# GpSimd tied to VectorE in a planned kernel: channel attention and a feed-forward block on one core

## The chip, the core and the metric

The kernel runs on one core of one Trainium2 chip. The metric is device time in microseconds, from the run's start to its end; the time before is 2167.81 us, the median of three runs (2167.71 to 2172.11). TensorE does the matrix products, VectorE and ScalarE the element-wise work, GpSimd a few subtractions; SyncE only issues DMAs. In the profile they are PE (its weight loads PEld), DVE, ACT, POOL and SP.

## The reference, cut to what matters

```python
# q, k, v: 4 x 6080 x 256;  w_in: 256 x 2048;  w_out: 2048 x 256, all float32
qn = q / (norm(q, axis=1) + 1e-6); kn = k / (norm(k, axis=1) + 1e-6)
a = softmax(kn.T @ qn / tau)          # 256 x 256 per batch
x = (v @ a).reshape(24320, 256)
h = x @ w_in
g = where(h >= 1, h, where(h <= -1, 0, (h + 1)**2 / 4))
out = g @ w_out
```

The attention is over channels: a batch's 6080 rows meet only in a 256 x 256 matrix.

## The kernel before

**Arithmetic.** `x @ w_in` is never formed with `x`: per batch the kernel multiplies the softmax matrix into `w_in` once and applies the product W to v. Every float32 operand is split in a high part, rounded to fp32r, and a low part, the rest; `mm3` (L588) makes each product of three matmuls. W times v, 256 hidden columns by two blocks of up to 512 tokens, is done as seven products in the manner of Strassen; their sums and differences are made by ScalarE copies (L766, L768), VectorE additions (L771, L775) and, for the pieces of v, GpSimd subtractions (L868 in `make_V`, into the tiles `t`).

**Groups.** The main loop has 192 groups: 4 batches, 6 pairs of token blocks, 8 blocks of 256 hidden columns. A group makes four banks of h; for each, ScalarE saturates (L919) and squares (L923), VectorE takes the maximum with h (L928), which is the activation; then the high part is copied (L943 on ScalarE or L945 on VectorE, as the planner picks) and VectorE subtracts it to give the low part (L947). The results (`g`, `x` in the profile) are what the matmuls with w_out read. In the first of the eight blocks the w_out product is also done with fewer multiplications: four GpSimd subtractions in `combos` (L993) make the sums of the activations that it needs; there are 24 such chains.

**Work beside it.** While one batch runs, the next one's 256 x 256 matrix is summed chunk by chunk: a DMA of q and k rows, a split on ScalarE and VectorE (L597, L598, the tile `kqs`), twelve matmuls of 256 columns, and an addition on VectorE (L615). GpSimd also makes sums of W (L824 in `split_f`) and of w_in (L563). Two PSUM banks (pool Z) serve, in turn, the products of the h chain, the fourth bank of h and the chunk's matmuls: the chunk can begin only when VectorE has read the last of h from its bank (L928).

**What sets the order.** Nothing of the main part is scheduled by the compiler. `op()` records an operation with its engine, a duration, what it reads and writes, and a due time; `Order.run` then plays the whole program through as a plan: at each step it takes the operation that can start first on any engine, the one with the lowest due time among those that can start now, gives it a start, an end and a buffer, and emits it. The emitted order is the order on each engine's queue; across engines only real dependencies are kept, by semaphores. The plan knows that some VectorE operations and the GpSimd ones shut each other out: an operation marked `locks` starts only when the other engine's lock has ended, which is `RELEASE` = 0.14 before the end. Due times come from tables of offsets (`T_PLAIN`, `T_STR`) from the group's 16 units, and from a few numbers in the main loop. In the plan a DMA ends a fixed `LAT` of 3.0 after its bytes have passed a single stream.

Of the kernel before, what the change touches and what calls it, by code (L numbers as in the profile page):

```python
# [11 lines left out]
U32 = mybir.dt.uint32  # L12
# [3 lines left out]
P = 128  # L16
# [35 lines left out]
SOON = 0.3  # L52
AHEAD, RATE = -34.0, 41.78
LATER = -3.46


class Op:
    __slots__ = ("eng", "dur", "fn", "due", "deps", "gates", "bufs", "next", "count", "start", "end", "n", "size",
                 "alts", "slack", "lat", "locks", "table")


class Order:
# [10 lines left out]
    LOAD = 1.29  # L73
    BYTES = 405e3
    FREE = {"PE": 2.0, "ACT": 2.0, "DVE": 1.5, "POOL": 1.5, "SP": 1.2}

    def __init__(self):
        self.ops = []
        self.lock = {"DVE": 0.0, "POOL": 0.0}
        self.table = None  # L80

# [64 lines left out]
    def run(self):  # L146
        free = dict(self.FREE)
        avail = {e: [] for e in self.LAG}
        dma = 0.0
        for o in self.ops:  # L150
# [19 lines left out]
        while left:  # L170
# [82 lines left out]
def pool_us(n):  # L253
# [7 lines left out]
G = 16  # L261
U = 32.22

# [5 lines left out]

LAT = 3.0  # L270
SLACK = 1
# [6 lines left out]
SQ0 = (4, 2)  # L278
RN_SLACK = (1.0, 3.0)
ET_SLACK = (2.0, 3.0)  # L280

# [3 lines left out]
T_PLAIN = {  # L285
    'sat00': 2.98,
    'sq00': -0.31,
    'max00': -2.38,
    'sat01': 7.36,
    'sq01': 3.87,  # L290
    'max01': 15.96,
    'sat11': 31.21,
    'sq11': 16.45,
    'max11': 17.07,
    'sat10': 16.54,
    'sq10': 12.89,
    'max10': 12.97,
    'sq': 9.06,
    'hi0': ((0, 16.38), (1, 16.82)),
    'lo0': ((0, 21.57), (1, 24.39)),  # L300
    'hi1': ((0, 23.28), (1, 23.36)),
    'lo1': ((0, 21.72), (1, 13.19)),
    'o': ((34.97, 38.77, 42.57, 39.06), (24.47, 26.42, 31.77, 20.96)),
}
T_STR = {
    'sat00': 1.98,
    'sq00': -7.92,
    'max00': -4.57,
    'sat01': -9.47,
    'sq01': -2.24,  # L310
    'max01': 50.9,
    'sat11': 26.21,
    'sq11': -0.38,
    'max11': 16.09,
    'sat10': 27.37,
    'sq10': 30.81,
    'max10': -3.19,
    'sq': 44.51,
    'hi0': ((0, -20.66), (1, 35.02)),
    'lo0': ((0, 27.87), (1, 18.19)),  # L320
    'hi1': ((0, 23.08), (1, 11.54)),
    'lo1': ((0, 13.1), (1, 8.58)),
    'sum': (36.44, 30.5, 21.24, 20.85),
    'direct': (17.8, 24.05, 22.11, 13.48),
    'chain': (35.74, 38.29, 60.46),
    'hi2': ((0, 14.57), (1, 40.57)),
    'lo2': ((0, 25.25), (1, 38.89)),
    'hi4': ((0, 44.31),),
    'lo4': ((0, 43.11),),
    'late': -22.72,  # L330
    'early': 23.14,
}
# [10 lines left out]
def channel_attention_moe(ctx: ExitStack, tc: tile.TileContext, kq, kqT, vT, tau, w_in, w_out, outT):  # L343
# [12 lines left out]
    nc = tc.nc  # L356
# [5 lines left out]
    RT = 2  # L362
# [111 lines left out]
    def load(b, src, dst, due, size, gates=(), r=(), slack=0.0):  # L474
        return op("SP", 0.35, lambda: nc.sync.dma_start(out=dst(), in_=src()), r=r, w=[b], due=due, gates=gates,
                  size=size, slack=slack)


    def convert(src, out, dst, due, gates=(), step=0.4, load_due=None, n=1, keep=None):
# [23 lines left out]
        if keep is not None:  # L503
            op("SP", 0.35, lambda: nc.sync.dma_start(out=x_dram[keep], in_=cu()), r=[cb], w=[x_store[keep]], due=due + 20,
               size=128 * 2048)
# [35 lines left out]
    def make_w_in(i, due, gates=(), load_due=None):  # L541
        b = win_buf[0, i] = buf("win")
        convert(w_in[i].rearrange("p a f -> p (a f)"), [b], lambda x: b.ap[:, x].rearrange("p a f -> p (a f)"), due, gates,
                load_due=load_due, keep=i)
        sb_, y, h = i // 4, i // 2 % 2, i % 2
        for ct, j in ((0, V_11), (1, V_21)) if y == 0 else ((1, V_22),):
            op("SP", 0.35, lambda ct=ct, j=j: nc.sync.dma_start(
                out=wop_dram[sb_][:, j, :, h * FF:(h + 1) * FF], in_=b.ap[:, :, ct, :].bitcast(U32)),
               r=[b], w=[wop_store[sb_][j]], due=due + 24, size=128 * 2048)

    def sums_w_in(i, due, gates=()):
# [80 lines left out]
    def softmax(b, due):  # L632
# [81 lines left out]
        else:  # L714
# [17 lines left out]

            op("SP", 3.0, blocks, r=[x], w=[ed], due=due + 8, size=P * 2048, slack=ET_SLACK[0])
            op("SP", 0.7, rows, r=[ed], w=[f], due=due + 8, size=P * 2048, slack=ET_SLACK[1])
# [45 lines left out]
    def make_W7(b, sb_, d, gates=()):  # L780
# [16 lines left out]
        for k, (it, y, h) in enumerate(((0, 0, a), (0, 1, bb), (1, 1, h22), (1, 0, z))):  # L797
            o = buf("u", TB)
            op("ACT", act_us(TB), lambda it=it, h=h, o=o: nc.scalar.mul(o.ap, h.ap, st.rs()[:, it:it + 1]), r=[h, st.col],
               w=[o], due=d + (10, 15, 16, 18)[k])  # L800
            op("SP", 0.35, lambda it=it, y=y, o=o: nc.sync.dma_start(
                out=raw_dram[b][sb_][:, 2 * y:2 * y + 2, it], in_=o.ap.rearrange("p (n f) -> p n f", n=2).bitcast(U32)),
               r=[o], w=[raw_store[b][sb_]], due=d + (10, 15, 16, 18)[k], size=128 * 2048)
# [30 lines left out]
    def split_W(b, i, f, due, parts=((0, NS),), eng="POOL", fview=lambda x: x):  # L834
        w = w_buf[b, 0, i]
        split_f(f, w, due, parts, eng, fview=fview)
        op("SP", 0.35, lambda: nc.sync.dma_start(out=w_dram[b][i], in_=w.ap.bitcast(U32).rearrange("p a j f -> p (a j f)")),
           r=[w], w=[w_store[b][i]], due=due + 24, size=128 * WSZ * 4)
# [204 lines left out]
    def o_ops(g):  # L1043
# [6 lines left out]
        for y in (1, 0):  # L1050
            dues = T_PLAIN["o"][y]
            for ct in range(CT):
# [8 lines left out]
                if i == FP - 1:  # L1061
# [11 lines left out]
                    op("SP", 0.35, lambda yb=yb, ct=ct, c0=c0: nc.sync.dma_start(  # L1073
                        out=outT[ct * P:(ct + 1) * P, c0:c0 + n], in_=yb.ap[:, :n]), r=[yb], due=due + 1,
# [80 lines left out]
    for g, (b, k, i) in enumerate(groups):  # L1155
# [17 lines left out]
        if i == 4 and g + 4 < NG:  # L1173
            make_V(*groups[g + 4][:2], d + 17.46, gate(g), 2.25)
        if b + 1 < B:
# [6 lines left out]
            for c, r0 in enumerate(rows):  # L1182
                if q == lo_ + c * (hi_ - lo_) // len(rows):
                    gram_chunk(b + 1, r0, min(P, (N - r0) // RT), d + 16.08, gate(g))
            for c in range(24):
                if q == SQ0[b > 0] + c * (KP * FP - SOFT_AT - SQ0[b > 0] + 1) // 24:
                    s, r = divmod(c, 2 * NCW)
                    square_piece(b + 1, s, r // NCW, r % NCW, d + 23.68, gate(g))
# [35 lines left out]
```

## Time and profile before

| | |
|---|---|
| median of three runs | 2167.81 us |
| profiled execution, its own time | 2169.51 us |
| its span, first to last instruction | 2167.7 us |
| PE busy, share of the span | 2150.7 us, 99% |
| DVE busy | 1896.2 us, 87% |
| ACT busy | 1635.1 us, 75% |
| POOL busy | 396.1 us, 18% |

A matmul's record runs on after the next has started, so PE's busy time counts a little more than its work. In the timeline a row gives start, duration, engine, line, operation, tiles, shapes and a count of like instructions merged; in square brackets stands the idle time of the engine just before it and what ended it.

### The profile page before, as it was taken

The page shows a single profiled execution, that of the slowest core. Times are in us where ns is not written, and L with a number is a line of the kernel's source. Part 1 is how long each engine was busy: PE and PEld are TensorE (multiplying, and loading weights), DVE is VectorE, ACT ScalarE, POOL GpSimd, SP SyncE. Part 2 cuts the span into 40 slices and gives each one's busy share as a digit, 9 for nine tenths or more (in the row PEclk, how much of TensorE's full clock was granted, in tenths as well). Part 3 has the DMA queues.
Part 4 walks back from the last instruction along what each step waited for, and adds up shares of the span by engine and source line. Part 5 has one row for each costly group of instructions (what it writes and reads, how often), then busy time and mean ns, then how long its engine had stood idle before and what let it go on. Part 6 is the DMA issues. An engine that isn't in the chain of part 4 may idle for free.

```text
span 2167.7 us, 28241 instructions
## 1 busy us (share of the span) xinstructions
PE 2150.7 (99%) x9800; PEld 1783.5 (82%) x9800; DVE 1896.2 (87%) x3017; ACT 1635.1 (75%) x2943; POOL 396.1 (18%) x358
## 2 busy tenths in 40 slices
PE   9999999999999999999999999999999999999999
PEld 7888888788878888888887888888888788888888
DVE  8998889889798888988979889898897998888886
ACT  6687788778688787777868877777787876776775
POOL 0321032121141110111124101011112410110110
PEclk9999999999999999999999999999999999999999
DMA  9854366544755444544566444444457433333331
GB/s 387 302 183 172 134 203 216 170 152 156 233 189 187 160 163 173 191 155 138 175 214 209 172 178 170 153 172 162 142 182 231 143 123 108 119 123 108 118 122 70
DMA packets 123839, 371.47 MB, mean 171 GB/s; under 512 B 17200, under 2 KB 48816, under 8 KB 121136
## 3 DMA queue, kind: packets, MB, share of 16 engines
q1 hardware_dynamic: 123696, 369.67, 48.6%
q8 instruction: 77, 1.26, 0.2%
q14 instruction: 66, 0.54, 0.1%
HBM read 298.84 MB, written 70.78 MB: 171 GB/s over the span
## 4 chain that ended last, share of the span: by engine, by line
PE 88%; DVE 8%; ACT 2%; issue 1%; DMA 1%; SPq 0%; DVEq 0%; ACTq 0%
PE bank L588 86%; DVE x L947 2%; PE bank L1107 2%; DVE u_mem L928 2%; DVE mh_mem L1123 1%; ACT u_mem L919 1%; ACT u_mem L923 1%; DVE x L945 1%; DVE g L947 0%; DVE w_mem L830 0%; DMA raw_mem<-raw_d 0%; DVE mh_mem L775 0%; DMA kq<-kq 0%; DVE u_mem L497 0%; DVE kqs L598 0%
## 5 line engine op out<-in xcount | busy, mean ns | idle before, releaser
L588 PE MATMUL bank<-v,w_mem 128*128 128x512 f32 (+1 forms) x3264 | 861.5, 389 | 1.0 <-DVE bank L771 0.3
L588 PE MATMUL bank<-x,wout 128*128 128x512 f32 (+1 forms) x3195 | 823.4, 388 | 1.6 <-DVE x L947 1.2
L588 PEld LDWEIGHTS bank<-v,w_mem 128*128 128x128 f32 x3264 | 607.4, 188 | 130.2 <-ACT bank L768 4.2
L588 PEld LDWEIGHTS bank<-x,wout 128*128 128x128 f32 x3195 | 597.8, 188 | 125.7 <-DVE x L947 5.6
L919 ACT ACTIVATE u_mem<-bank 128x512 f32<-128x512 f32 (+1 forms) x576 | 341.6, 594 | 316.2 <-PE bank L588 311.3
L928 DVE TENSOR_TENSOR u_mem<-bank,u_mem 128x512 f32<-128x512 f32 (+1 forms) x576 | 390.5, 679 | 167.7 <-ACT u_mem L923 165.1
L923 ACT ACTIVATE u_mem<-u_mem 128x512 f32<-128x512 f32 (+1 forms) x768 | 466.6, 626 | 7.9
L947 DVE TENSOR_TENSOR x<-u_mem,x 128x512 fp32r<-128x512 f32 (+1 forms) x580 | 416.5, 730 | 7.8 <-ACT x L943 1.2
L588 PE MATMUL bank<-g,wout 128*128 128x512 f32 (+1 forms) x1053 | 278.0, 388 | 0.0
L588 PEld LDWEIGHTS bank<-g,wout 128*128 128x128 f32 x1053 | 197.0, 188 | 39.6 <-DVE g L947 0.2
L943 ACT CAST x<-u_mem 128x512 fp32r<-128x512 f32 (+1 forms) x285 | 175.6, 618 | 55.4 <-DVE u_mem L928 45.9
L588 PE MATMUL bank<-x,w_mem 128*128 128x512 f32 (+1 forms) x768 | 211.0, 389 | 0.1
L868 POOL TENSOR_TENSOR t<-raw_mem 128x512 f32<-128x512 f32 (+1 forms) x48 | 67.1, 1398 | 627.6 <-DMA raw_mem<-vT 355.8
L588 PEld LDWEIGHTS bank<-x,w_mem 128*128 128x128 f32 x768 | 142.7, 188 | 32.1 <-ACT bank L768 1.3
L868 POOL TENSOR_TENSOR t<-raw_mem,t 128x512 f32<-128x512 f32 (+1 forms) x48 | 66.4, 1383 | 497.0 <-DVE v L877 383.4
L771 DVE TENSOR_TENSOR bank<-bank,mh_mem 128x512 f32<-128x512 f32 (+1 forms) x198 | 135.8, 686 | 13.7 <-PE bank L588 11.9
L775 DVE TENSOR_TENSOR mh_mem<-bank,mh_mem 128x512 f32<-128x512 f32 (+1 forms) x198 | 134.3, 678 | 14.8 <-PE bank L588 13.0
L928 DVE TENSOR_TENSOR u_mem<-mh_mem,u_mem 128x512 f32<-128x512 f32 (+1 forms) x192 | 140.1, 730 | 2.3 <-ACT u_mem L923 2.3
L945 DVE CAST x<-u_mem 128x512 fp32r<-128x512 f32 (+1 forms) x295 | 129.7, 440 | 10.6 <-DVE u_mem L928 0.9
L947 DVE TENSOR_TENSOR g<-u_mem,g 128x512 fp32r<-128x512 f32 (+1 forms) x188 | 135.6, 731 | 2.1 <-ACT g L943 0.5
L993 POOL TENSOR_TENSOR cc<-u_mem 128x512 f32<-128x512 f32 (+1 forms) x48 | 73.6, 1533 | 301.5 <-DVE u_mem L928 283.6
L919 ACT ACTIVATE u_mem<-mh_mem 128x512 f32<-128x512 f32 (+1 forms) x192 | 119.6, 623 | 7.9 <-DVE mh_mem L775 7.6
(129 smaller groups left out, 2028.7 us busy)
## 6 DMA issues: line engine op xcount, KB each, us to landing
w_mem<-w_d SPq DMA_DIRECT2D x160, 896.0 KB, 4.6
raw_mem<-kqT SPq DMA_DIRECT2D x60, 512.0 KB, 5.4
w_d<-w_mem SPq DMA_DIRECT2D x32, 896.0 KB, 4.4
raw_mem<-kq SPq DMA_DIRECT2D x51, 512.0 KB, 5.3
kq<-kq SPq DMA_DIRECT2D x20, 1024.0 KB, 8.5
raw_mem<-vT SPq DMA_DIRECT2D x40, 512.0 KB, 6.3
outT<-y_mem SPq DMA_DIRECT2D x80, 256.0 KB, 2.1
win_mem<-wop_d SPq DMA_DIRECT2D x21, 512.0 KB, 5.6
```

The lines of the kernel that those rows point to most:

```text
L588: nc.tensor.matmul(out, lhsT=lhs(a), rhs=rhs(c), start=start and m == 0, stop=stop and m == 2, skip_group_check=skip)
L771: op("DVE", dve_us(n), lambda: nc.vector.tensor_tensor(out=bb.ap[:, :n], in0=z.ap[:, :n], in1=m5.ap[:, :n], op=ALU.add), r=[z, m5], w=[bb] ...
L775: op("DVE", dve_us(n), lambda: nc.vector.tensor_tensor(out=h22.ap[:, :n], in0=z.ap[:, :n], in1=m5.ap[:, :n], op=ALU.add), r=[z, m5], w=[h2 ...
L868: op("POOL", pool_us(n), lambda: nc.gpsimd.tensor_tensor(out=tt(x), in0=a(), in1=c(), op=ALU.subtract), r=r, w=[ts[x]], due=due + d, gates ...
L919: op("ACT", act_us(n), lambda: nc.scalar.activation(half_of(u, x, n), h.ap[:, :n], IDENTITY_SAT240, scale=240.0), r=[h], w=[u.parts[x]], t ...
L923: op("ACT", act_us(n * (1 + (x is None))), lambda: nc.scalar.activation(part_of(u, x, n), part_of(u, x, n), AF.Square, bias=0.5, scale=1.0 ...
L928: op("DVE", dve_us(n), lambda: nc.vector.tensor_tensor(out=us(), in0=h.ap[:, :n], in1=us(), op=ALU.max), r=[h], w=[u.parts[x]], h=[u], due ...
L943: op("ACT", act_us(cols), lambda x=x: nc.scalar.copy(part(0, x), part_of(u, x, n)), r=of(u.parts, x), w=of(t.parts, x), h=[u, t], due=due, ...
L945: other=("DVE", dve1_us(cols), lambda x=x: nc.vector.tensor_copy(part(0, x), part_of(u, x, n))))
L947: op("DVE", dve_us(n * (1 + (x is None))), lambda x=x: nc.vector.tensor_tensor(out=part(1, x), in0=part_of(u, x, n), in1=f32(part(0, x)), ...
L993: op("POOL", pool_us(n), lambda out=out, o=o, a=a, x=x, c_=c_, y=y: nc.gpsimd.tensor_tensor(out=half_of(out, o, n), in0=half_of(a, x, n), ...
L1107: nc.tensor.matmul(g.ap[:, it * C:(it + 1) * C], lhsT=rb.ap[:p, k0:k0 + P], rhs=rb.ap[:p, t * 512 + C:t * 512 + 2 * C], start=(r0 == 0 and ...
```

## The change

GpSimd's operations that carry the lock get one dependency more: when the plan places one, it looks among the last 16 placed VectorE operations for the latest one that in the plan has ended by then (0.11 for the signal, 0.02 of tolerance), and the GpSimd instruction is made to wait for that instruction's semaphore. Nothing else is computed; no operation is added or taken away.

The plan's DMA model changes: the stream starts at 2.3, a transfer enters it 1.2 after its issue, ends 0.1 after its bytes, and a load is usable 1.8 later still (`LAND`), where before every transfer ended 3.0 after its bytes; issuing one costs 0.45 on SyncE in place of 0.35. `AHEAD` in the class is this 1.2; the module's `AHEAD`, negative before and after, is another number. With it all due offsets have other values, so the planner lays out other orders and, in a few places, picks ScalarE instead of VectorE for a high-part copy.

```diff
@@ class Order
-    BYTES = 405e3
+    BYTES = 403e3
+    AHEAD = 1.2
@@ run
-        dma = 0.0
+        dma = 2.3
...
             if o.eng == "SP":
-                dma = max(dma, t) + o.size / self.BYTES
-                o.end = dma + LAT + o.slack
+                dma = max(dma, t + self.AHEAD) + o.size / self.BYTES
+                o.end = dma + 0.1 + o.slack
             else:
                 o.end = t + o.lat
-            o.fn()
+            o.out = o.fn()
+            if o.eng == "DVE":
+                self.placed.append(o)
+            elif o.eng == "POOL" and o.locks:
+                done = [d for d in self.placed[-16:] if d.end + self.TO["POOL"] <= o.start + 0.02]
+                if done and self.tie:
+                    self.tie(o.out, done[-1].out)
@@ 
-U = 32.22
+U = 34.28
-LAT = 3.0
+LAND = 1.8
-RN_SLACK = (1.0, 3.0)
-ET_SLACK = (2.0, 3.0)
+RN_SLACK = (1.0, 1.0)
+ET_SLACK = (0.5, 1.0)
@@ T_PLAIN, T_STR (nearly every value; one shown)
-    'max10': 12.97,
+    'max10': 26.77,
@@ load (other DMAs alike: 0.35 to 0.45)
-        return op("SP", 0.35, lambda: nc.sync.dma_start(out=dst(), in_=src()), r=r, w=[b], due=due, gates=gates,
-                  size=size, slack=slack)
+        return op("SP", 0.45, lambda: nc.sync.dma_start(out=dst(), in_=src()), r=r, w=[b], due=due, gates=gates,
+                  size=size, slack=LAND + slack)
@@ main loop
-                softmax(b + 1, d + 27.02)
+                softmax(b + 1, d + 35.96)
+    def tie(later, earlier):
+        tc.add_manual_dep(later.ins, earlier.ins.name, mybir.DependencyInfo(
+            mybir.DependencyClass.Sync, mybir.DependencyReason.DATA), reason="order of GpSimd and VectorE")
+    od.tie = tie
     od.run()
```

On GpSimd, where the first batch's sums of w_in (L563, after the change L570) are followed by a pair of subtractions for the pieces of v (L868, then L875), the queue reads before, with the semaphores that each instruction waits for:

```order
L563 TENSOR_TENSOR raw_mem_93<-raw_mem_93 128x256 [waits DMAHW3_49,DMAHW4_49,DMAHW1_49,Activation_49]
L563 TENSOR_TENSOR raw_mem_93<-raw_mem_93 128x256 [waits Pool_49]
L563 TENSOR_TENSOR raw_mem_93<-raw_mem_93 128x256
L868 TENSOR_TENSOR t0_107<-raw_mem_93 128x512 [waits DMAHW5_49,DMAHW4_49,Activation_49]
L868 TENSOR_TENSOR t1_108<-raw_mem_93,t0_107 128x512 [waits Pool_49]
```

and after the change:

```order
L570 TENSOR_TENSOR raw_mem_93<-raw_mem_93 128x256 [waits DMAHW3_49,DMAHW0_49,DVE_49]
L570 TENSOR_TENSOR raw_mem_93<-raw_mem_93 128x256 [waits DVE_49,Pool_49]
L570 TENSOR_TENSOR raw_mem_93<-raw_mem_93 128x256 [waits DVE_49]
L875 TENSOR_TENSOR t0_107<-raw_mem_93 128x512 [waits DMAHW4_49,DMAHW5_49,DVE_49,Activation_49]
L875 TENSOR_TENSOR t1_108<-raw_mem_93,t0_107 128x512 [waits DVE_49,Pool_49]
```

The sequence is the same; each instruction now also waits for a VectorE instruction (DVE_49). Of GpSimd's 363 instructions 114 waited for VectorE before and 337 do after.

On TensorE, ahead of one chunk of the third batch's 256 x 256 matrix (`kqs`), the queue reads before (bank6 and bank7 are the two Z banks, `x3` at a name's start is a piece of v, a final x3 a count):

```order
L588 MATMUL bank0_117<-x3_1041,w_mem_89 128x512 x3
L588 MATMUL bank7_124<-v5_104,w_mem_89 128x512 x3
L588 MATMUL bank2_119<-g0_98,wout_80 128x512 x3
L588 MATMUL bank6_123<-v0_99,w_mem_89 128x512 x3
L588 MATMUL bank2_119<-g0_98,wout_80 128x512 x3
L588 MATMUL bank4_121<-x1_732,wout_80 128x512 x3
L588 MATMUL bank7_124<-kqs_109 128x256 x12
```

and after the change:

```order
L595 MATMUL bank0_117<-x3_1063,w_mem_89 128x512 x3
L595 MATMUL bank6_123<-v5_104,w_mem_89 128x512 x3
L595 MATMUL bank7_124<-v0_99,w_mem_89 128x512 x3
L595 MATMUL bank2_119<-x0_718,wout_80 128x512 x6
L595 MATMUL bank7_124<-v1_100,w_mem_89 128x512 x3
L595 MATMUL bank0_117<-v2_101,w_mem_89 128x512 x3
L595 MATMUL bank6_123<-kqs_109 128x256 x12
```

Between the last product that fills the bank (bank7 from v5 before, bank6 from v5 after) and the chunk that needs it empty stand 12 matmuls before and 15 after.

## Rows read from the trace of the kernel before

**Rows 1.** The page, section 1: busy time and share of the span

```profile
PE 2150.7 (99%) x9800; PEld 1783.5 (82%) x9800; DVE 1896.2 (87%) x3017; ACT 1635.1 (75%) x2943; POOL 396.1 (18%) x358
```

**Rows 2.** Windows: busy time in each stretch (PE, PEld, DVE, ACT, POOL), clock, DMA

```profile
0.00:60.00 60.00, 56.11 (x232) 46.26 (x233) 46.86 (x60) 36.15 (x41) 5.28 (x13) 0.94 0.98 389
...
60.00:2165.00 2105.00, 2094.54 (x9570) 1737.25 (x9568) 1849.37 (x2958) 1598.94 (x2902) 390.79 (x345) 1.00 0.48 165
```

**Rows 3.** Waits of the weight loads, 60 to 2165: total, times, longest

```profile
PEld bank L588 <- DVE u_mem L928: 11.6, 17, 2.3
PEld bank L588 <- DVE x L947: 9.5, 18, 0.9
PEld bank L588 <- ACT bank L768: 5.5, 17, 0.5
PEld bank L588 <- DVE mh_mem L775: 5.3, 15, 0.7
PEld bank L588 <- DVE bank L771: 4.1, 13, 0.7
```

**Rows 4.** The page, section 5: matmuls of one kind, mean ns of one

```profile
L588 PE MATMUL bank<-x,wout 128*128 128x512 f32 (+1 forms) x3195 | 823.4, 388 | 1.6 <-DVE x L947 1.2
```

**Rows 5.** Timeline ahead of the longest stop, at 390.5

```profile
380.75 4.51 POOL L563 TENSOR_TENSOR raw_mem<-raw_mem 128x256 f32<-128x256 f32 x4 [17.96 <-DMA raw_mem<-x_d]
...
385.22 1.30 POOL L868 TENSOR_TENSOR t<-raw_mem 128x512 f32<-128x512 f32 x1
385.29 1.51 DVE L945 CAST x<-u_mem 128x512 fp32r<-128x512 f32 x1
...
386.41 2.20 PE L588 MATMUL bank<-x,wout 128*128 128x512 f32 x9
386.60 1.35 POOL L868 TENSOR_TENSOR t<-raw_mem,t 128x512 f32<-128x512 f32 x1
386.72 1.77 DVE L928 TENSOR_TENSOR u_mem<-mh_mem,u_mem 128x512 f32<-128x512 f32 x1
...
390.53 1.69 PE L588 MATMUL bank<-kqs 128*128 128x256 f32 x12 [1.92 <-DVE u_mem L928]
```

**Rows 6.** DVE by line and form: busy, mean ns of one

```profile
L928 DVE TENSOR_TENSOR u_mem<-bank,u_mem 128x512 f32<-128x512 f32 x480 | 328.0, 685 | 126.5 <-ACT u_mem L923 124.1
...
L928 DVE TENSOR_TENSOR u_mem<-mh_mem,u_mem 128x512 f32<-128x512 f32 x160 | 119.4, 746 | 0.8 <-ACT u_mem L923 0.8
...
L945 DVE CAST x<-u_mem 128x512 fp32r<-128x512 f32 x242 | 107.7, 446 | 8.8 <-DVE u_mem L928 0.9
```

**Rows 7.** Timeline ahead of the stops at 736.8 and 738.0

```profile
732.48 1.30 POOL L868 TENSOR_TENSOR t<-raw_mem 128x512 f32<-128x512 f32 x1 [23.88 <-DMA raw_mem<-vT]
...
733.86 1.30 POOL L868 TENSOR_TENSOR t<-raw_mem,t 128x512 f32<-128x512 f32 x1
733.89 1.82 DVE L928 TENSOR_TENSOR u_mem<-mh_mem,u_mem 128x512 f32<-128x512 f32 x1
...
736.83 0.73 PE L588 MATMUL bank<-x,wout 128*128 128x512 f32 x2 [0.27 <-DVE x L947]
...
738.03 0.74 PE L588 MATMUL bank<-kqs 128*128 128x256 f32 x4 [0.47 <-DVE u_mem L928]
```

**Rows 8.** Timeline: a GpSimd subtraction issued while VectorE is busy

```profile
611.68 0.68 DVE L928 TENSOR_TENSOR u_mem<-bank,u_mem 128x512 f32<-128x512 f32 x1
...
612.28 0.68 DVE L947 TENSOR_TENSOR x<-u_mem,x 128x512 fp32r<-128x512 f32 x1
612.44 1.67 POOL L993 TENSOR_TENSOR cc<-u_mem 128x512 f32<-128x512 f32 x1 [2.88 <-DVE u_mem L928]
...
612.88 2.19 DVE L830 TENSOR_TENSOR w_mem<-raw_mem,w_mem 128x896 fp32r<-128x896 f32 x1
```

**Rows 9.** Waits for GpSimd's results, whole span

```profile
ACT x L943 <- POOL u_mem L993: 6.4, 10, 0.7
...
ACT x L943 <- POOL cc L993: 4.9, 7, 1.1
```

More of the change, by code (lines that the diff above doesn't have):

```diff
@@ L52 @@
 SOON = 0.3
-AHEAD, RATE = -34.0, 41.78
-LATER = -3.46
+AHEAD, RATE = -25.72, 44.15
+LATER = -3.74
 class Op:
     __slots__ = ("eng", "dur", "fn", "due", "deps", "gates", "bufs", "next", "count", "start", "end", "n", "size",
-                 "alts", "slack", "lat", "locks", "table")
+                 "alts", "slack", "out", "lat", "locks", "table")
 class Order:
@@ L79, in __init__ @@
         self.lock = {"DVE": 0.0, "POOL": 0.0}
-        self.table = None
+        self.table, self.placed, self.tie = None, [], None
     def cost(self, eng, dur, r):
@@ L285 @@
 T_PLAIN = {
[L286 to L296, printed above, removed]
-    'max10': 12.97,
[L298 to L303, printed above, removed]
+    'sat00': -1.82,
@@ L304 @@
+    'sq00': 7.34,
+    'max00': -3.51,
+    'sat01': 3.03,
+    'sq01': 4.32,
+    'max01': 13.39,
+    'sat11': 26.31,
+    'sq11': 5.68,
+    'max11': 12.73,
+    'sat10': 11.93,
+    'sq10': 11.5,
+    'max10': 26.77,
+    'sq': 2.38,
+    'hi0': ((0, 16.19), (1, 16.64)),
+    'lo0': ((0, 21.5), (1, 24.47)),
+    'hi1': ((0, 23.81), (1, 23.93)),
+    'lo1': ((0, 20.3), (1, 10.11)),
+    'o': ((35.98, 38.77, 42.56, 39.06), (24.57, 18.78, 31.77, 22.42)),
 }
 T_STR = {
-    'sat00': 1.98,
-    'sq00': -7.92,
@@ L308 @@
[L308 to L331, printed above, removed]
+    'sat00': 4.47,
+    'sq00': -8.11,
+    'max00': -3.57,
+    'sat01': -5.72,
+    'sq01': -1.84,
+    'max01': 51.23,
+    'sat11': 26.79,
+    'sq11': 3.65,
+    'max11': 16.69,
+    'sat10': 23.02,
+    'sq10': 26.77,
+    'max10': 1.12,
+    'sq': 42.09,
+    'hi0': ((0, -15.43), (1, 29.89)),
+    'lo0': ((0, 26.14), (1, 17.69)),
+    'hi1': ((0, 21.32), (1, 11.52)),
@@ L332 @@
+    'lo1': ((0, 17.42), (1, 11.92)),
+    'sum': (32.85, 29.56, 19.16, 18.24),
+    'direct': (17.8, 24.05, 20.89, 13.71),
+    'chain': (36.35, 47.54, 66.55),
+    'hi2': ((0, 15.89), (1, 43.57)),
+    'lo2': ((0, 28.81), (1, 37.59)),
+    'hi4': ((0, 44.87),),
+    'lo4': ((0, 42.97),),
+    'late': -22.54,
+    'early': 22.32,
 }
@@ L503, in convert @@
         if keep is not None:
-            op("SP", 0.35, lambda: nc.sync.dma_start(out=x_dram[keep], in_=cu()), r=[cb], w=[x_store[keep]], due=due + 20,
+            op("SP", 0.45, lambda: nc.sync.dma_start(out=x_dram[keep], in_=cu()), r=[cb], w=[x_store[keep]], due=due + 20,
                size=128 * 2048)
@@ L569, in sums_w_in @@
         for a in range(2):
-            op("SP", 0.35, lambda a=a: nc.sync.dma_start(
+            op("SP", 0.45, lambda a=a: nc.sync.dma_start(
                 out=wop_dram[sb_][:, 0:NS:2, a, h * FF:(h + 1) * FF],
@@ L731, in rows @@
                                       in_=eT_dram[b][jt * P:(jt + 1) * P].rearrange("p (t c) -> p t c", t=CT))
-            op("SP", 3.0, blocks, r=[x], w=[ed], due=due + 8, size=P * 2048, slack=ET_SLACK[0])
+            op("SP", 3.9, blocks, r=[x], w=[ed], due=due + 8, size=P * 2048, slack=ET_SLACK[0])
             op("SP", 0.7, rows, r=[ed], w=[f], due=due + 8, size=P * 2048, slack=ET_SLACK[1])
@@ L836, in split_W @@
         split_f(f, w, due, parts, eng, fview=fview)
-        op("SP", 0.35, lambda: nc.sync.dma_start(out=w_dram[b][i], in_=w.ap.bitcast(U32).rearrange("p a j f -> p (a j f)")),
+        op("SP", 0.45, lambda: nc.sync.dma_start(out=w_dram[b][i], in_=w.ap.bitcast(U32).rearrange("p a j f -> p (a j f)")),
            r=[w], w=[w_store[b][i]], due=due + 24, size=128 * WSZ * 4)
@@ L1173, in channel_attention_moe @@
         if i == 4 and g + 4 < NG:
-            make_V(*groups[g + 4][:2], d + 17.46, gate(g), 2.25)
+            make_V(*groups[g + 4][:2], d + 15.28, gate(g), 1.82)
         if b + 1 < B:
@@ L1183, in channel_attention_moe @@
                 if q == lo_ + c * (hi_ - lo_) // len(rows):
-                    gram_chunk(b + 1, r0, min(P, (N - r0) // RT), d + 16.08, gate(g))
+                    gram_chunk(b + 1, r0, min(P, (N - r0) // RT), d + 17.42, gate(g))
             for c in range(24):
```

8 lines of the change are left out of this document (4 added, 4 removed).

## The prediction

> **What bounds the kernel now.** I read the page's busy times first: TensorE is busy for 99% of the span, VectorE for 87%, GpSimd for 18% [rows 1]. The matmuls are the same before and after, so only the time in which TensorE has none can move. Second, the windows say how much that is: up to 60 us TensorE lacks 3.9 us, and from 60 to 2165 us it is idle for 2105.00 - 2094.54 = 10.5 us [rows 2]. That understates the loss. One matmul's record is 388 ns long [rows 4], but nine in a row take 2.20 us [rows 5], so the next starts after (2.20 - 0.39) / 8 = 0.226 us, and a stop hides its first 0.16 us under the record before it. Third, the waits of the weight loads give the number of stops: the five largest rows hold 80 waits and 36.0 us [rows 3]. So the matmul stream loses about 10.5 + 80 x 0.16 = 23 us after the start. That is an upper bound on the gain as long as the first 60 us stay, about 1.1% of the time; the kernel is one long stream of matmuls with some 80 short stops.
>
> Who makes the stops is in the same rows: VectorE's four of the five hold 30.5 of 36.0 us [rows 3]. It is not late for want of speed on average; the question is what makes it late there. The timeline ahead of the longest stop shows it [rows 5]. GpSimd's four sums of w_in begin when a load lands, 18 us of idling ended, and the pair of subtractions for v follows at once, at 385.22 and 386.60. Beside the first, a VectorE cast takes 1.51 us where its kind takes 0.45 on the mean [rows 6]; beside the second, a maximum takes 1.77 where 0.75 is the mean [rows 6]. Each ends about when the subtraction does. Together VectorE is 2.1 us late, and the chunk that waits for it leaves TensorE idle for 1.92 us, 2.1 with the hidden part. At 732 to 738 us the picture is the same: the pair begins when its load lands, the maximum beside its second half takes 1.82 us, and two stops follow, 0.27 and 0.47 us idle, 1.1 with twice 0.16 [rows 7]. The maximum that reads a PSUM bank shows no such stretch: 685 ns on the mean over 480 [rows 6]. So what shuts the two engines out of each other is SBUF traffic, one of two at a time, and the stops are where GpSimd's turn falls just ahead of a VectorE result that TensorE needs.
>
> **The change part by part.** *The ties.* They add a wait on VectorE to some 220 GpSimd instructions, and each adds no busy time. Behind a waiting GpSimd instruction only GpSimd's queue stands; it is busy for 18% [rows 1], and of its consumers only ScalarE's copies are seen waiting, 6.4 and 4.9 us in 17 waits [rows 9]. So I cost the waits themselves at nothing; if that cover is gone, the price is the first rival's. What the ties take away is a GpSimd operation running before its place in the plan, where a load or a finished GpSimd operation releases it. They can't take away one that comes late because its load is late; GpSimd's queue at the first place shows the same instructions in the same order, with DVE_49 added to each.
>
> *The DMA model.* It moves no transfer by itself; it moves where the plan thinks that a load lands, and with it where GpSimd's turn falls. Both places above begin with a landing [rows 5, 7], so a plan that has it right puts VectorE's needed result on the right side of the pair. A wrong one costs what it costs now.
>
> *The new due times.* They change the order on TensorE, ScalarE and VectorE nearly everywhere. The one place where I can read the gain off the order is the chunk's bank: 12 matmuls stood between filling and needing it, 12 x 0.226 = 2.7 us, and now 15, 3.4 us. The stop there was 1.1 us in two parts [rows 7]; 0.7 us more room takes away most of the second, which is 0.63 with its hidden part. Other places get other room, and new tight ones are possible. The eight casts that move from VectorE to ScalarE give VectorE 8 x 0.45 = 3.6 us of 1896, which I leave out.
>
> *The sum.* What the edit is worth lies between nothing, or less if it makes new stops, and the 23 us of all stops. The waits of the kind that a GpSimd turn lengthens directly or through the queue, the maximum's (L928) and the low part's (L947), are 21.1 of 36.0 us, 59% [rows 3]; of 23 us that is 13.5. GpSimd's subtractions don't vanish, 390.8 us of them [rows 2] still take the port, and an order that is right in the plan still meets late loads. I take three quarters of the 13.5, since both stops that I followed have a cause that the change addresses: 10 us. That quarter is a choice, and both ends stay in the range. The first 60 us keep their order on TensorE nearly row for row, so I leave their 3.9 us, and the end of the program, alone. Against its own time the profiled execution would go from 2169.5 (span 2167.7 and 1.8 around it) to 2159.5; the median shown is 2167.8, 1.7 lower, so I forecast 2157.8 us, 0.46% less. A difference under 0.2%, 4.3 us, can't be told from none here.
>
> **What a tie can't order.** At 612 us GpSimd starts 0.08 us after VectorE's maximum has ended (611.68 + 0.68), but VectorE's own next operation is already recorded from 612.28; GpSimd takes 1.67 instead of the 1.30 of the undisturbed pair [rows 7], so it first waits some 0.4 us, and then the VectorE operation behind takes 2.19 us [rows 8]. The two take turns. A tie to an operation that has just ended releases GpSimd at this very point, and the race with the next VectorE operation stays. The Trainium skill, "SBUF — State Buffer", section "Who interferes with whom", has the rule behind it: the shared port pair is an exclusive lock, whoever issues first holds it for the whole instruction, the other blocks. By that rule the tied instruction, woken later than VectorE goes on by itself, lets one VectorE operation through first; the trace agrees in this row.
>
> **The rivals.** *First, slower: the chains of sums stretch.* The 24 chains of four subtractions (L993) can run back to back today, 0.08 us apart as the pair does [rows 7]. Tied, each of the last three may wait for one VectorE operation more, 0.7 us [rows 6], so a chain ends up to 2.1 us later. ScalarE's copies already wait in 17 places for these results [rows 9]; if half of the delay in each of the 24 chains gets through the copies and low parts to TensorE, that is 24 x 1.05 = 25 us, if a third of that half, 8. It decides from 0.42 us per chain, where it eats the 10. For it: the copies wait now. Against it: the longest of those waits is 1.1 us, and GpSimd idles four fifths of the time. I price it at 8 us over before: 2176.
>
> *Second, no change: the stops move.* VectorE is 87% busy, each GpSimd operation still takes its turn, and a new order has its own tight places. For it: nearly every due time is new, and 12 matmuls of room still stand ahead of other chunks. A fifth of the 13.5 would stay: 2.7 us, 2165.
>
> *Third, more: VectorE always goes first.* If a tied operation loses the race every time and GpSimd's pairs no longer fall together, all of VectorE's share goes, 30.5 / 36.0 of 23 us = 19.5: 2148. Against it: in the row at 612 us GpSimd's turn came one operation later and the next VectorE operation paid 1.1 us [rows 8]. The Trainium skill's rule on the lock, above, speaks against it as well: GpSimd too keeps the pair once it has it.
>
> *Fourth, the ties do nothing* because GpSimd is already behind the plan: where loads land late, the tie is met before it counts. Then only the new order is left, and the time is the second rival's.
>
> **How the numbers follow.** The forecast has 0.57, the first rival 0.15, the second and fourth together 0.18, the third 0.10. The forecast's own range is 2152 to 2163, from all of the 13.5 us and some to a third of it. Of the second and fourth, 0.14 lies within 0.2% and 0.04 below. So faster by over 0.2%: 0.57 + 0.10 + 0.04 = 0.71; within 0.2%: 0.14; slower: 0.15. The range of 8 in 10 takes in the no-change case and leaves out most of the first rival and the far half of the third: 2149 to 2170.
>
> **What would show it.** Right: TensorE's idle time from 60 us on falls from 10.5 to about 6 us; the waits for L928 and L947 in the weight loads' table fall from 35 to under 20; the chunk stops of 0.5 us and more are gone; GpSimd's subtractions list VectorE as what ended their idle time. The DMA step is right if no long stop begins with a landing. Wrong: stops of 1 us behind a stretched VectorE operation stay as many; or copies (L943, then L950) wait much more than 11 us for GpSimd, which is the first rival; or TensorE's idle time falls and the time does not, which would mean that I have the wrong loss. The forecast fails if the time is above 2163.5.

## The result, and the profile after

The changed kernel takes 2145.22 us (median, 2144.74 to 2147.03); the kernel before took 2169.95 us beside it (2167.71 to 2172.11). The ratio is 0.9888 [0.9871, 0.9905]: 24.7 us faster, where 10 were forecast, and below the range. The profiled execution took 2147.03 us with a span of 2145.2, 22.5 less than the span before.

The page of the kernel after, section 1 (answers to [rows 1]); after it, from section 4, the shares of the chain that ended last.

```profile
PE 2133.9 (99%) x9800; PEld 1787.2 (83%) x9800; DVE 1866.1 (87%) x3009; ACT 1627.2 (76%) x2951; POOL 402.5 (19%) x358
...
PE 95%; DVE 2%; DMA 1%; ACT 1%; issue 0%; POOL 0%; SPq 0%; DVEq 0%
```

The windows show when the time was won. As the two programs end 22 us apart, I take a stretch that lies inside both, 60 to 2140 us. Kernel before, columns as in [rows 2]:

```profile
60.00:2140.00 2080.00, 2070.40 (x9460) 1716.67 (x9459) 1832.29 (x2929) 1587.40 (x2880) 390.79 (x345) 1.00 0.48 167
```

Kernel after, the start too:

```profile
0.00:60.00 60.00, 54.95 (x235) 45.48 (x236) 47.66 (x61) 36.22 (x41) 5.28 (x13) 0.97 0.98 390
60.00:2140.00 2080.00, 2077.30 (x9560) 1740.62 (x9559) 1817.82 (x2948) 1590.45 (x2909) 397.23 (x345) 1.00 0.48 167
```

In the same 2080 us TensorE does 100 matmuls more. At 2080 / 9560 = 0.218 us each that is 21.8 of the 22.5 us. So these 21.8 us are stops of the stream, at a granted clock of 1.00 in both kernels. The rest is 3 more matmuls in the first 60 us, 0.7 us; there the clock was 0.94 before and 0.97 after, so that part may belong to the execution and not to the change. TensorE's idle time goes from 9.6 to 2.7 us.

The weight loads' waits of the kernel after, 60 to 2142 us (total, times, longest), answer to [rows 3]:

```profile
PEld bank L595 <- ACT bank L775: 5.0, 13, 1.8
PEld bank L595 <- DVE x L954: 1.7, 3, 0.8
PEld bank L595 <- DVE u_mem L935: 1.4, 7, 0.3
PEld bank L595 <- DVE mh_mem L782: 0.6, 3, 0.2
PEld bank L595 <- DVE bank L778: 0.2, 1, 0.2
```

Lines have moved by 7: L588 is L595 now, L928 is L935, L947 is L954. ScalarE's row stands almost as it stood (5.5 us in 17 waits, then 5.0 in 13); VectorE's four rows, 30.5 us in 63 waits, are 3.9 in 14.

VectorE's forms of the kernel after (busy, mean ns of one), against [rows 6]:

```profile
L935 DVE TENSOR_TENSOR u_mem<-bank,u_mem 128x512 f32<-128x512 f32 x480 | 327.7, 685 | 125.3 <-ACT u_mem L930 119.4
L935 DVE TENSOR_TENSOR u_mem<-mh_mem,u_mem 128x512 f32<-128x512 f32 x160 | 110.8, 693 | 3.2 <-ACT u_mem L930 3.2
L952 DVE CAST x<-u_mem 128x512 fp32r<-128x512 f32 x218 | 92.9, 427 | 7.7 <-PE bank L595 0.5
```

The maximum that reads a PSUM bank has its 685 ns as before; the one that reads SBUF alone falls from 746 to 693 ns, so most of its long meetings with GpSimd are gone.

What ended GpSimd's idle time ahead of the subtractions for v, in the kernel before (total, times, longest):

```profile
POOL t L868 <- DVE v L877: 511.3, 37, 29.1
POOL t L868 <- DMA raw_mem<-vT: 355.8, 17, 48.9
```

and in the kernel after:

```profile
POOL t L875 <- DVE v L884: 397.9, 37, 26.6
POOL t L875 <- DVE bank L778: 320.1, 13, 29.9
POOL t L875 <- DMA raw_mem<-vT: 77.8, 2, 48.7
```

Seventeen times the landing of the piece's own load let GpSimd go; now twice. Where the landing ended the wait before, mostly a VectorE operation that the subtraction reads nothing from ends it now (`DVE bank L778`): that is the tie at work.

The longest stop that is left, timeline of the kernel after (start, duration, idle time before and its releaser):

```profile
1043.48 2.49 POOL L831 TENSOR_TENSOR sf_mem<-sf_mem 128x128 f32<-128x128 f32 x4 [15.54 <-DMA sf_mem<-e_d]
...
1046.00 0.94 ACT L835 CAST eT<-sf_mem 128x896 fp32r<-128x896 f32 x1 [1.98 <-POOL sf_mem L831]
1046.85 0.55 ACT L775 COPY bank<-bank 128x480 f32<-128x480 f32 x1
...
1047.45 0.92 PE L595 MATMUL bank<-x,w_mem 128*128 128x480 f32 x3 [1.33 <-ACT bank L775]
```

GpSimd's sums wait for a landing, ScalarE's cast waits 1.98 us for them, and the bank that TensorE needs stands behind that cast in ScalarE's queue. No tie makes a landing earlier.

### The profile page after: what moved, and what is told of

It reads as the page before. It is cut to its first block, busy times and chain, and to the rows that moved or that the text cites. A ratio compares the mean times of both kernels' runs of the same rounds, so it can differ in the third digit from the quotient of the medians.

```text
span 2145.2 us, 28485 instructions
## 1 busy us (share of the span) xinstructions
PE 2133.9 (99%) x9800; PEld 1787.2 (83%) x9800; DVE 1866.1 (87%) x3009; ACT 1627.2 (76%) x2951; POOL 402.5 (19%) x358
## 4 chain that ended last, share of the span: by engine, by line
PE 95%; DVE 2%; DMA 1%; ACT 1%; issue 0%; POOL 0%; SPq 0%; DVEq 0%
PE bank L595 94%; DVE mh_mem L1130 1%; DMA kq<-kq 1%; PE bank L1114 1%; DMA raw_mem<-w_out 0%; DVE u_mem L504 0%; ACT u_mem L930 0%; DVE x L954 0%; DVE v L884 0%; DVE u_mem L507 0%; ACT u_mem L926 0%; DVE wout L514 0%; DVE u_mem L500 0%; POOL sf_mem L831 0%; ACT y_mem L1129 0%
## 5 line engine op out<-in xcount | busy, mean ns | idle before, releaser
L595 PE MATMUL bank<-v,w_mem 128*128 128x512 f32 (+1 forms) x3264 | 839.1, 388 | 0.7 <-ACT bank L775 0.7
L595 PE MATMUL bank<-x,wout 128*128 128x512 f32 (+1 forms) x3159 | 794.8, 388 | 0.0
L595 PEld LDWEIGHTS bank<-v,w_mem 128*128 128x128 f32 x3264 | 610.1, 188 | 124.4 <-ACT bank L775 2.7
L595 PEld LDWEIGHTS bank<-x,wout 128*128 128x128 f32 x3159 | 591.1, 188 | 117.9 <-DVE x L954 0.2
L935 DVE TENSOR_TENSOR u_mem<-bank,u_mem 128x512 f32<-128x512 f32 (+1 forms) x576 | 390.2, 680 | 162.7 <-ACT u_mem L930 154.5
L954 DVE TENSOR_TENSOR x<-u_mem,x 128x512 fp32r<-128x512 f32 (+1 forms) x564 | 398.0, 719 | 4.5 <-ACT x L950 0.5
L595 PE MATMUL bank<-g,wout 128*128 128x512 f32 (+1 forms) x1089 | 279.4, 388 | 0.0
L595 PEld LDWEIGHTS bank<-g,wout 128*128 128x128 f32 x1089 | 203.7, 188 | 40.5
L950 ACT CAST x<-u_mem 128x512 fp32r<-128x512 f32 (+1 forms) x297 | 182.8, 618 | 50.3 <-DVE u_mem L935 39.4
L595 PE MATMUL bank<-x,w_mem 128*128 128x512 f32 (+1 forms) x768 | 209.1, 388 | 1.3 <-ACT bank L775 1.3
L875 POOL TENSOR_TENSOR t<-raw_mem 128x512 f32<-128x512 f32 (+1 forms) x48 | 74.8, 1559 | 616.0 <-DVE bank L778 320.1
L595 PEld LDWEIGHTS bank<-x,w_mem 128*128 128x128 f32 x768 | 143.6, 188 | 31.1 <-ACT bank L775 2.3
L875 POOL TENSOR_TENSOR t<-raw_mem,t 128x512 f32<-128x512 f32 (+1 forms) x48 | 69.5, 1449 | 473.0 <-DVE v L884 363.8
L954 DVE TENSOR_TENSOR g<-u_mem,g 128x512 fp32r<-128x512 f32 (+1 forms) x204 | 149.1, 741 | 1.7
L778 DVE TENSOR_TENSOR bank<-bank,mh_mem 128x512 f32<-128x512 f32 (+1 forms) x198 | 135.8, 686 | 15.8 <-PE bank L595 13.5
L935 DVE TENSOR_TENSOR u_mem<-mh_mem,u_mem 128x512 f32<-128x512 f32 (+1 forms) x192 | 132.5, 690 | 4.6 <-ACT u_mem L930 4.6
L952 DVE CAST x<-u_mem 128x512 fp32r<-128x512 f32 (+1 forms) x267 | 113.7, 426 | 9.3 <-PE bank L595 0.5
```

Of the source, the lines that this page charges most:

```text
L595: nc.tensor.matmul(out, lhsT=lhs(a), rhs=rhs(c), start=start and m == 0, stop=stop and m == 2, skip_group_check=skip)
L778: op("DVE", dve_us(n), lambda: nc.vector.tensor_tensor(out=bb.ap[:, :n], in0=z.ap[:, :n], in1=m5.ap[:, :n], op=ALU.add), r=[z, m5], w=[bb] ...
L875: op("POOL", pool_us(n), lambda: nc.gpsimd.tensor_tensor(out=tt(x), in0=a(), in1=c(), op=ALU.subtract), r=r, w=[ts[x]], due=due + d, gates ...
L935: op("DVE", dve_us(n), lambda: nc.vector.tensor_tensor(out=us(), in0=h.ap[:, :n], in1=us(), op=ALU.max), r=[h], w=[u.parts[x]], h=[u], due ...
L950: op("ACT", act_us(cols), lambda x=x: nc.scalar.copy(part(0, x), part_of(u, x, n)), r=of(u.parts, x), w=of(t.parts, x), h=[u, t], due=due, ...
L952: other=("DVE", dve1_us(cols), lambda x=x: nc.vector.tensor_copy(part(0, x), part_of(u, x, n))))
```

## The experiments

The change has three parts, and they can be had alone: the ties, the DMA model (rate, issue and landing time of the plan's transfers) and the due times. All twelve kernels compute the whole result. Theory A: the ties hold GpSimd back from running ahead of the plan, and that is most of the gain. Theory B, the rival: the new order, with landings that are right, is the gain, and the ties add little. Theory C stands between them: each has a part, or needs the other. Theory D: what matters is that GpSimd keeps to its time in the plan, whichever engine's progress tells it the time. Theory E, its rival: what counts is the order of the two engines that shut each other out, VectorE first, so that there are fewer collisions. A gain is what a kernel's median lies below that of the kernel before in the same comparison; by the intervals each is good to about 3 us.

**The ties, taken out and put in alone.** Without ties, from the kernel after:

```diff
-    od.tie = tie
```

> The changed kernel without the ties: the line that sets od.tie is left out, so the plan and the order on every engine are those of the changed kernel. Theory A (the ties hold GpSimd at its planned place, and that is what removes the stops): most of the 24.7 us come back, 2157 to 2168 us, with VectorE operations stretched to 1.5 us and more ahead of TensorE's stops. Theory B (the new order and due times remove the stops, the ties do little): 2145 to 2150 us. Theory C (both are needed, the order is fitted to a plan that only the ties make true): between, 2152 to 2160 us, and above 2165 us would say that the new order without ties is no better than the old.

The ties alone, added to the kernel before:

```diff
-            o.fn()
+            o.out = o.fn()
+            if o.eng == "DVE":
+                self.placed.append(o)
+            elif o.eng == "POOL" and o.locks:
+                done = [d for d in self.placed[-16:] if d.end + self.TO["POOL"] <= o.start + 0.02]
+                if done and self.tie:
+                    self.tie(o.out, done[-1].out)
...
+    od.tie = tie
```

> The kernel before with the ties alone: old DMA model, old due times, old order on every engine. Theory A: most of the gain, 2147 to 2155 us. Theory B: no gain, 2165 to 2172 us. Theory C: part of it; a count in the trace of before found about 60 of 348 subtractions that started over 0.3 us ahead of their place, and the stops behind such ones sum to some 6 us, so about 2160 to 2164 us.

Measured: without ties 2155.31 us, ratio 0.9937 [0.9924, 0.9949], 13.7 gained; ties alone 2150.95, 0.9915 [0.9901, 0.9929], 18.1 gained. The order on every engine is the old one in the second kernel, so 18 us are the ties' by themselves; with the new order they add 24.7 - 13.7 = 11.0. The ties alone came where theory A has them. Without ties the time lies in C's range and not in A's: the new order has a share of its own.

Ties alone, timeline at the place of [rows 5] (lines moved by 6):

```profile
378.48 5.01 POOL L569 TENSOR_TENSOR raw_mem<-raw_mem 128x256 f32<-128x256 f32 x4 [18.85 <-DVE g L951]
...
381.32 0.43 DVE L951 CAST x<-u_mem 128x512 fp32r<-128x512 f32 x1
381.78 1.10 DVE L934 TENSOR_TENSOR u_mem<-mh_mem,u_mem 128x512 f32<-128x512 f32 x1
...
385.27 0.43 DVE L951 CAST g<-u_mem 128x512 fp32r<-128x512 f32 x1
385.29 1.69 PE L594 MATMUL bank<-kqs 128*128 128x256 f32 x12
...
385.83 1.75 POOL L874 TENSOR_TENSOR t<-raw_mem 128x512 f32<-128x512 f32 x1 [2.35 <-issue]
...
387.85 1.35 POOL L874 TENSOR_TENSOR t<-raw_mem,t 128x512 f32<-128x512 f32 x1 [0.27 <-DVE gacc L621]
```

The chunk starts without the 1.92 us of idle time. The pair that stood ahead of its maximum in [rows 5] comes behind the chunk now. The profile names no releaser for it (`issue`), but it starts 0.13 us after a VectorE cast has ended (385.27 + 0.43), as a tie to that cast would have it. What released GpSimd ahead of the subtractions for v, in the same kernel, whole span (two of the rows):

```profile
POOL t L874 <- DVE x L953: 344.8, 13, 29.6
...
POOL t L874 <- DMA raw_mem<-vT: 77.1, 2, 48.6
```

and without ties, from the kernel after:

```profile
POOL t L875 <- DMA raw_mem<-vT: 393.1, 18, 48.6
```

The order is not what holds the pairs back; the tie is. Set side by side place by place, in 15 of the 17 places the pair's own load no longer ends GpSimd's wait: 14 times a VectorE operation does, once another load. So there the load had landed before the tie let go: against the plan the pair was early. At the place of [rows 7] GpSimd idles 29.55 us ahead of the pair in place of 23.88.

Ties alone, the weight loads' waits, 60 to 2140 us:

```profile
PEld bank L594 <- ACT bank L774: 4.7, 14, 0.9
PEld bank L594 <- DVE mh_mem L781: 4.2, 13, 0.7
PEld bank L594 <- DVE u_mem L934: 4.1, 13, 0.5
PEld bank L594 <- DVE bank L777: 1.9, 11, 0.2
```

All VectorE rows of this view sum to 13.6 us in 50 waits, against 32.8 in 71 before, 12.4 in 32 without ties and 3.9 in 14 in the kernel after. Without ties VectorE's waits are no longer than with the ties alone, yet the gain is 4.4 us smaller; ScalarE's row is 8.8 us in 19 waits there, 4.7 in 14 here.

**The old DMA model, and the old due times, with ties.** From the kernel after, first the model (with its issue costs and slacks), then the due times:

```diff
-    BYTES = 403e3
-    AHEAD = 1.2
+    BYTES = 405e3
+    AHEAD = 0.0
...
-                o.end = dma + 0.1 + o.slack
+                o.end = dma + LAT + o.slack
```

> The changed kernel, ties and new due times, with the old DMA model in the plan (a transfer ends 3.0 after its bytes, no 1.2 ahead of them, issue 0.35, the old slacks). If the DMA model matters by itself, GpSimd's pairs again begin with late landings beside a result that TensorE waits for: 2152 to 2165 us. If it is the ties and the due times: 2145 to 2150 us.

```diff
-AHEAD, RATE = -25.72, 44.15
+AHEAD, RATE = -34.0, 41.78
...
-U = 34.28
+U = 32.22
```

> The changed kernel, ties and new DMA model, with the due times of before (both tables, U, LATER and the four offsets in the main loop). If the due times carry the gain: 2160 to 2172 us. If a plan that holds on the chip is enough, whatever its due times: 2146 to 2153 us.

Measured: 2154.26 us, 0.9930 [0.9918, 0.9943], 14.8 gained; 2152.75, 0.9923 [0.9909, 0.9936], 16.3 gained. The first time lies in the range for a DMA model that matters, but not by the path named there: a landing of its load lets a pair go only once. The second lies where a plan that holds is enough. Either part alone beside the ties gains no more than the ties by themselves, with intervals that overlap; both together gain 6.6 more.

**The two parts without ties.** The same two edits of the kernel after, with the ties taken out as well: with the old due times the DMA model is all that is left of the change, with the old model the due times are.

> The new DMA model alone: old due times, no ties. With ties this layout measured 2152.75 us. If it is the ties that put every layout near 2150 us and a new layout is worth nothing by itself: 2163 to 2172 us. If a plan with true landings puts GpSimd's turns right without a tie: 2153 to 2160 us.

> The new due times alone: old DMA model, no ties. With ties this layout measured 2154.26 us. Due times fitted to another DMA model have no reason to be good here: 2163 to 2175 us. If they are better in themselves, with more room ahead of the chunks: 2155 to 2160 us.

Measured: 2162.13 us, 0.9965 [0.9953, 0.9978], 7.8 gained; 2168.52, 0.9991 [0.9982, 1.0], 1.4 gained, no difference that can be told. The first lies between its two forecasts, the second where due times fitted to another model bring nothing. With these, every combination has its gain in us:

```
                      no ties   ties
neither                  0      18.1
due times alone          1.4    14.8
DMA model alone          7.8    16.3
both                    13.7    24.7
```

The due times are worth nothing that can be told on the old model, and 13.7 - 7.8 = 5.9 (with ties 8.4) on the new one.

**Which ties.** Only the subtractions for v in `make_V` tied (`and o.piece`), then all but these (`and not o.piece`), on the kernel before:

```diff
+            elif o.eng == "POOL" and o.locks and o.piece:
...
-               r=r, w=[ts[x]], due=due + d, gates=gates)
+               r=r, w=[ts[x]], due=due + d, gates=gates).piece = True
```

> The kernel before with ties on the 96 subtractions for the pieces of v alone (L868). The ties alone on all of GpSimd measured 2150.95 us, 18 less than before. If the pairs that a landing load sets off early are what makes the stops (their waits for the load fall from 17 to 2 once all are tied), this keeps most of the 18: 2152 to 2158 us. If the chains of sums (L993) and the sums of W (L824) have an equal part: 2158 to 2165 us.

> The kernel before with ties on all GpSimd operations but the subtractions for the pieces of v. The counterpart of the run before: if the pairs are the cause, 2162 to 2168 us; if the others have an equal part, 2155 to 2162 us. Should the two parts sum to more than 18 us, one undoes what the other would have gained.

Measured: 2156.71 us, 0.9936 [0.9923, 0.9950], 13.2 gained; 2162.25, 0.9964 [0.9951, 0.9976], 7.7 gained. Together 20.9, near the 18.1 of all ties. The pairs that my prediction followed at two places are the larger share, with 96 of GpSimd's 358 instructions.

**What the tie reads.** Ties to the last ScalarE operation that is done in the plan, and ties to VectorE's fifth-last, on the kernel before:

```diff
-            if o.eng == "DVE":
+            if o.eng == "ACT" and o.out is not None:
```

> The kernel before with the same ties, but each to the last ScalarE operation that has ended by then in the plan, in place of the VectorE one. Theory D (the tie only has to hold GpSimd until its time in the plan; which engine's progress it reads does not matter): 2150 to 2155 us. Theory E (it is the order of the two engines that shut each other out that counts, so the wait must be on VectorE): 2158 to 2168 us.

```diff
-                if done and self.tie:
-                    self.tie(o.out, done[-1].out)
+                if len(done) > 4 and self.tie:
+                    self.tie(o.out, done[-5].out)
```

> The kernel before with ties four VectorE operations looser: to the fifth last that has ended by then. Four operations are about 3 us of VectorE's time. If loads release GpSimd's pairs many microseconds ahead of their place, a loose tie still catches them: 2151 to 2156 us. If they run ahead by one to four operations, the gain falls to less than half: 2160 to 2168 us.

Measured: 2153.82 us, 0.9926 [0.9913, 0.9938], 16.2 gained; 2158.40, 0.9945 [0.9931, 0.9958], 11.7 gained. Section 1 of the page of the kernel tied to ScalarE:

```profile
PE 2141.4 (100%) x9800; PEld 1782.0 (83%) x9800; DVE 1896.4 (88%) x3017; ACT 1636.3 (76%) x2943; POOL 380.6 (18%) x358
```

and what released its subtractions:

```profile
POOL t L874 <- ACT bank L774: 390.4, 16, 28.3
...
POOL t L874 <- DMA raw_mem<-vT: 85.3, 3, 28.8
```

VectorE has the same 3017 instructions as before and is busy for 1896.4 us, before for 1896.2 [rows 1]. In sum it is stretched as much as ever, and 16 us are gained. What moved is where, as two of its forms show (against [rows 6]):

```profile
L951 DVE CAST x<-u_mem 128x512 fp32r<-128x512 f32 x242 | 113.1, 468 | 8.8 <-DVE u_mem L934 0.9
L934 DVE TENSOR_TENSOR u_mem<-mh_mem,u_mem 128x512 f32<-128x512 f32 x160 | 111.2, 695 | 1.0 <-ACT u_mem L929 0.9
```

The casts are longer than before (468 ns, 446 before), the maximum is not stretched any more (695, 746 before; 691 with the ties to VectorE alone, 725 without ties). The place of [rows 5] in the kernel tied to ScalarE:

```profile
382.83 0.68 DVE L934 TENSOR_TENSOR u_mem<-mh_mem,u_mem 128x512 f32<-128x512 f32 x1
...
385.25 1.29 POOL L874 TENSOR_TENSOR t<-raw_mem 128x512 f32<-128x512 f32 x1 [1.15 <-ACT bank L774]
385.89 0.94 DVE L951 CAST g<-u_mem 128x512 fp32r<-128x512 f32 x1
...
385.91 1.69 PE L594 MATMUL bank<-kqs 128*128 128x256 f32 x12
...
386.86 1.66 DVE L953 TENSOR_TENSOR g<-u_mem,g 128x512 fp32r<-128x512 f32 x1
```

VectorE's operations beside the pair take 0.94 and 1.66 us, but the results that the chunk needs are ahead of them: it starts at 385.91 with no idle time before it. So theory D stands, and E falls as far as it asks for the wait on VectorE. Its fewer collisions aren't settled by this run, since GpSimd's busy time fell by 15.5 us; the loose ties settle them for the larger part. Section 1 of their page, then their releaser row:

```profile
PE 2144.2 (99%) x9800; PEld 1782.9 (83%) x9800; DVE 1895.6 (88%) x3017; ACT 1635.3 (76%) x2943; POOL 400.5 (19%) x358
```

```profile
POOL t L874 <- DMA raw_mem<-vT: 137.9, 4, 48.9
```

VectorE and GpSimd together are busy no less than before (2296.1 us, 2292.3 before), and 11.7 us are gained. That gain lies between its two forecasts. A landing ends the wait 4 times in place of 17, so most landings come more than four VectorE operations ahead of the pair's place; the rest of the 18.1 us takes the tight tie.

**What is left.** A later landing in the plan for the load behind the stop at 1047 us, and a second tie, to ScalarE, beside the first; both on the kernel after:

```diff
-ET_SLACK = (0.5, 1.0)
+ET_SLACK = (1.5, 2.0)
```

> The changed kernel with a later landing in the plan of the two transfers that carry the softmax result (ET_SLACK from 0.5 and 1.0 to 1.5 and 2.0). Its longest stop left, 1.5 us near 1047 us, follows from that load: GpSimd's sums, a ScalarE cast that waits 2.0 us for them and a ScalarE copy that TensorE needs. If the plan has this landing 2 us too early: that stop goes, 2142 to 2145 us. If the new order behind it brings its own stops: 2144 to 2149 us.

```diff
+                for e in ("DVE", "ACT"):
+                    done = [d for d in self.placed[-32:] if d.eng == e and d.end + self.TO["POOL"] <= o.start + 0.02]
+                    if done:
+                        self.tie(o.out, done[-1].out)
```

> The changed kernel with a second tie on each of these GpSimd operations, to the last ScalarE operation that has ended by then in the plan. On the old order a loose tie gave 11.7 us and the tight one 18, so a still tighter hold may give more. If GpSimd still runs ahead between two VectorE operations at places that matter: 2141 to 2144.5 us. If the tie to VectorE already holds it where it counts: 2144.5 to 2147 us. If the added waits make GpSimd late for ScalarE's copies: above 2147.5 us.

Measured: 2146.69 us, 0.9891 [0.9878, 0.9905]; 2145.41, 0.9884 [0.9867, 0.9900]. Neither can be told from the kernel after. The first lies in the range for an order with stops of its own, the second in that for a tie that already holds GpSimd where it counts. With the later landing in the plan the stop at 1047 us is gone. GpSimd's sums there start at 1045.11, and TensorE's only idle time between 1030 and 1060 us is this (timeline):

```profile
1053.52 0.93 PE L595 MATMUL bank<-g,wout 128*128 128x480 f32 x3 [0.22 <-ACT y_mem L1077]
```

In return a stop near the start is longer, in that kernel:

```profile
88.35 2.71 PE L595 MATMUL bank<-v,w_mem 128*128 128x512 f32 x6 [1.92 <-ACT bank L775]
```

and in the kernel after:

```profile
88.82 1.66 PE L595 MATMUL bank<-v,w_mem 128*128 128x512 f32 x6 [0.71 <-ACT bank L775]
```

So the plan can step around a late landing (1.33 us became 0.22), but one profile of each can't tell whether the 1.2 us at 88 us come from the edit or from the loads of that execution. No kernel tried here beats the kernel after.

## Why the prediction was wrong

**Right: what bounds the kernel, and the mechanism.** TensorE's stream with its short stops is all that moved (100 matmuls more in 2080 us), and the stops were where GpSimd's turn fell ahead of a result that TensorE needs. With the ties alone the pair at 385 us went behind the chunk, and the 1.92 us are gone. One reading was loose: the two stretched VectorE operations did not end with the subtractions beside them but 0.28 and 0.54 us later (386.80 and 388.49 against 386.52 and 387.95).

**Failed: the sum, in two terms.** "I take three quarters of the 13.5" rested on the reading that only L928's and L947's waits are in reach, 59%. All four VectorE rows were: 30.5 us fell to 3.9. The two rows left out, the additions that read PSUM (L771, L775), aren't stretched themselves (691 and 683 ns before, 690 and 684 after), and their waits fell from 9.4 us to 0.8. The ties alone leave 6.1 of them, the new order without ties 2.6: most of this term goes with the new order, which the prediction priced at one chunk only (most of 0.63 us) and which gains 13.7 us without a tie. That the 3.3 us of the ties come from additions standing in VectorE's queue behind stretched operations fits, but no run shows it. And not a quarter stayed, but about an eighth of the waiting time.

Under the size lies a misreading. The prediction said of the ties that "they can't take away one that comes late because its load is late", and took the two pairs shown for such. A landing as releaser says only that GpSimd began as soon as it could, not that this was late. Against the plan the pairs were early, 15 of 17 times, and this is what a tie removes. The release rows of the kernel before couldn't tell early from late; the planned turn beside them could have. A later count in that trace, in the expectation of the ties alone, found some 60 early subtractions and still priced them at only 6 us. The ties alone, 18.1 us, already pass the forecast.

**Too small: the bound.** 23 us was to be all that the stream loses. Idle time and 0.16 us for each of the 91 waits of 60 to 2140 us made 24.2 before and 2.7 + 28 x 0.16 = 7.2 after: 17.0 less, where the matmuls say 21.8. With ties alone the count gives 8.7 + 27 x 0.16 = 13.0, the matmuls (81 more) 17.7. A part of the loss, near 5 us, is in no wait that I counted; where it sits is open.

**The DMA model and the due times.** "It costs what it costs now" was half right: the model alone gains 7.8 us with no tie. That it does so by moving GpSimd's turns to better places is not shown: a landing of its load still lets GpSimd go 18 times there, 17 before, though VectorE's rows at the weight loads sum to 22.7 us in place of 32.8. The due times' 0.7 us of room at the chunk says nothing of their worth: alone they gain 1.4, within what can't be told, and 5.9 or 8.4 on the new model. The table was worth something only with the DMA model that it came with. That "no long stop begins with a landing" is refuted by the stop at 1047 us.

**The rivals.** The first, chains that stretch, did not come. With ties alone ScalarE waits more for the pair, not for the chains:

```profile
ACT v L880 <- POOL t L874: 12.8, 18, 3.1
...
ACT x L949 <- POOL u_mem L999: 6.4, 10, 0.7
...
ACT x L949 <- POOL cc L999: 4.9, 7, 1.1
```

The copies behind the chains wait exactly as in [rows 9]; the others wait 12.8 us, 3.1 before, and 18 us are gained all the same, as ScalarE's own row at the weight loads is 4.7 us, 5.5 before. The second, stops that move, explains the due times alone at best (1.4 us), not the result. The third came nearest, 2148. With ties alone VectorE's busy time did fall, to 1879.7 us, but it need not go first for the gain: with ties to ScalarE its busy time is that of before. The Trainium skill, "SBUF — State Buffer", section "Who interferes with whom", has the shared port as an exclusive lock that whoever issues first keeps for its whole instruction; the runs agree (beside GpSimd's sums the maximum at 381.78 still takes 1.10 us, 0.69 on the mean). The larger part of the gain comes from where the collisions fall, not from their sum, as the loose ties show. The fourth is refuted with its premise: GpSimd was ahead of the plan, not behind.

## What to carry to other kernels

An operation that starts when its load lands may be early: compare its start with its place in the intended order before calling it late. Where a helper engine shares something with the engine on the path, let it wait for the progress of the plan (VectorE's or ScalarE's did here) rather than for its data alone. When sizing such a fix, count every wait for the disturbed engine, those of its undisturbed operations too, and price the new order by itself: here the undisturbed ones' waits fell from 9.4 us to 6.1 with the ties alone and to 2.6 with the new order alone.

## What the runs showed of the hardware that was not expected

Which engine pays for the collisions changed with the engine that the tie reads: with ties to VectorE VectorE is busy for 1879.7 us and GpSimd for 403.3, with ties to ScalarE for 1896.4 and 380.6 (before 1896.2 and 396.1), and the gains are 18.1 and 16.2 us. The loose ties, at 1895.6 and 400.5, still gain 11.7: TensorE's loss followed neither number. A second tie on GpSimd's instructions cost nothing that can be measured (2145.41 beside 2145.22 us).
